# Line-aligned tiles and a batch pipeline for the first chunk of a fused retention and GELU-MLP kernel

## The chip, the cores and the metric

The kernel runs on one core of a Trainium2 chip. The time is the device time of one execution in microseconds (us); a kernel is compared by the median of its timed runs. Engines are named as in the profile: PE multiplies matrices (PEld is its weight load), DVE, ACT and POOL do elementwise work, SP only issues DMAs. ACT and POOL issue DMAs as well, from the same instruction stream as their elementwise work, so such an issue stands in the way of what comes behind it.

## The reference

```python
def _attn_ref(q, k, v):                       # 4 batches, 8 heads, 768 steps, head size 64
    gamma = 1.0 - 2.0 ** (-5.0 - np.arange(H))
    scale = 1.0 / np.sqrt(D)
    for t in range(S):
        state = gamma * state + k_t (outer) v_t       # per batch and head, 64 x 64
        y[:, :, t] = scale * (q_t @ state)

def _moe_ref(x, w_in, w_out):                 # x: 3072 x 512, d_ff = 2048
    h = x @ w_in
    g = gelu_tanh(h)
    return g @ w_out
```

A decayed recurrent attention produces `x` (3072 tokens of 512 values), and a two-layer MLP with a tanh GELU is applied to each token.

## The kernel before

**Tiling.** The sequence is cut into 6 chunks `c` of 128 steps; each chunk has 4 batches `b`. The recurrence is done by chunks: inside a chunk as a masked attention, between chunks through a state `st` (f16) that is carried per batch. The 8 heads go as 4 pairs, one pair filling the 128 partitions.

**One batch of one chunk** is a chain that alternates between PE and the elementwise engines:

- `load1` brings q, k and v from HBM as 128 x 8 x 64 f32 tiles (256 KB each, in rows of 256 bytes).
- `prep1` scales q and k by the decay and casts all three to f16 (`q16`, `k16`, `v16`), at line 141 (q, k) and line 136 or 138 (v).
- `mm_T` transposes q and k on PE (L171) and `ev_T` copies the result out of PSUM (`qkT`, L163 on ACT, L165 on DVE).
- `mm_A` forms the scores (L189, 8 matmuls into two PSUM tiles) and `ev_A` masks them out into `a_sb` (L202, two DVE instructions).
- `mm_Y` forms the output `y_ps` (L212 from the state, L222 from the scores) and the state's increment `s_ps` (L234); `ev_Y` copies y into `xT`, the MLP's input (L163 or L165); `ev_S` updates `st` (L251 in chunk 0, L253 later, two DVE instructions); `decay` multiplies the state for the next chunk into `stg` on POOL (L262).

The PSUM tiles of T, A (two), Y and S all come from one ring of three buffers (tag `att`): each new tile waits until the third one before it has been copied out.

**The MLP.** `moe1(c, fc)` multiplies all 4 batches of a chunk (512 tokens) by one 128-column block `fc` of `w_in` (16 blocks, 4 matmuls each, L316) and applies the GELU on ACT (L325). It can be done for half of the tokens (256 columns, batches 0 and 1, or 2 and 3). `moe2` multiplies by `w_out` (L336), and `ev_O` writes the output. `w_in` lies in five tiles of 2, 2, 4, 4 and 4 blocks, `w_out` in four; POOL issues their loads, which cast f32 to f16.

**The order** is written out by hand; each engine runs its own instructions in the order in which the code emits them. `spin(n)` emits `n` matmuls of a zero tile by itself, 512 columns wide (L108), whose result is not used.

- *Chunk 0* (lines 394 to 426): after 16 spins, batch 0 is started; then each turn of the loop over `b` = 1 to 3 emits prep, `spin(5)`, `mm_T` of batch `b`, `mm_Y` of `b - 1`, the evictions on ACT, `mm_A` and `ev_A` of `b`, then `ev_S` and `decay` of `b - 1`. In turn 2 POOL first copies one element of the loaded q tile of batch 3, so that it waits for it, and then issues the five loads of `w_in`. Loads: ACT issues q and v of batch 0 and q of batch 1, SP all the others, in order of the batches.
- Then `moe1` for the first two blocks and batches 0 and 1, `mm_Y` of batch 3, blocks 2 and 3 for the first half, blocks 0 to 3 for the second half, and blocks 4 to 15 for all tokens.
- `hold` (L86) writes one element of the tile of q of chunk 1, batch 0, with a value of `w_in` tile 3: the loads of chunk 1 wait on SP until that tile has landed. Then POOL prepares chunk 1 and issues the loads of `w_out`; the loads of chunk 2 are held in the same way until `w_out` tile 2 is there.
- *Chunk 1*: T and A of batch 0 lie between blocks 14 and 15, then T1, Y0, A1 and Y1 follow one another, and T2 to Y3 are spread over `moe1` of chunk 1's first half. Later chunks are spread over the MLP of the chunk before.

**Addresses.** In the compiled kernel the tile `zero` starts at byte 17408 of each partition (68 x 256). The tile `warm`, two bytes wide, comes behind it, and every tile after that starts 32 bytes past a multiple of 256: the first q tile at 67616 (264 x 256 + 32), for instance.

Of the kernel before, what the change touches and what calls it, by code (L numbers as in the profile page):

```python
# [9 lines left out]
F16 = mybir.dt.float16  # L10
F32 = mybir.dt.float32
AF = mybir.ActivationFunctionType
# [4 lines left out]
def kernel(  # L17
# [9 lines left out]
    nc = tc.nc  # L27
    B, H, S, Dh = q.shape
# [5 lines left out]
    NF = d_ff // 128  # L34
# [12 lines left out]
    cst_h = nc.inline_tensor(cst_np, name="rr_cst")  # L47
# [4 lines left out]
    const = ctx.enter_context(tc.tile_pool(name="const", bufs=1))  # L52
# [6 lines left out]
    psum = ctx.enter_context(tc.tile_pool(name="psum", bufs=1, space=bass.MemoryType.PSUM))  # L59

    OQ, OK, OG, OT = 0, H, 2 * H, 2 * H + NHP
    cst = const.tile([128, OT + 128], F32)
    iden = const.tile([128, 128], F16)
    scr = const.tile([1, 4], F32)

    raw = {}
    srcs = {"q": q, "k": k, "v": v}
# [1 line left out]
    def ld_tile(nm, c, b):  # L69
        if (nm, c, b) not in raw:  # L70
            raw[nm, c, b] = ld.tile([128, H, Dh], F32, tag=f"{nm}32", name=f"{nm}32")
        return raw[nm, c, b]

    def load1(eng, nm, c, b):
        eng.dma_start(
            out=ld_tile(nm, c, b),
            in_=srcs[nm][b, :, c * C:(c + 1) * C, :].rearrange("h p d -> p h d"),
        )

    def load(c, b):  # L80
        for nm in "qkv":
            load1(nc.sync, nm, c, b)
# [2 lines left out]

        nc.gpsimd.tensor_copy(out=ld_tile(nm, c, b)[0:1, 0, 0:1], in_=until)  # L86

    nc.sync.dma_start(out=cst, in_=cst_h.ap())
    load1(nc.scalar, "q", 0, 0)
    load1(nc.sync, "k", 0, 0)  # L90
    load1(nc.scalar, "v", 0, 0)
    nc.sync.dma_start(out=iden, in_=iden_h.ap())
    load1(nc.scalar, "q", 0, 1)
    load1(nc.sync, "k", 0, 1)
    load1(nc.sync, "v", 0, 1)
    load(0, 2)
    load(0, 3)


    zero = const.tile([128, 512], F16, name="zero")  # L100
    nc.vector.memset(zero, 0.0)  # L101
    warm = const.tile([128, 1], F16)
    nc.scalar.activation(out=warm, in_=zero[:, 0:1], func=AF.Gelu_apprx_tanh, scale=1.0)

    def spin(n):
        ps = psum.tile([128, 512], F32, tag="o", bufs=2, name="spin_ps")
        for _ in range(n):
            nc.tensor.matmul(  # L108
                out=ps, lhsT=zero[:, 0:128], rhs=zero, start=True, stop=True
            )  # L110
# [20 lines left out]
    def prep1(eng, nm, c, b):  # L131
        t = pre.tile([128, H, Dh], F16, tag=f"{nm}16", name=f"{nm}16")
        src = raw[nm, c, b]
        if nm == "v":
            if eng is nc.scalar:
                eng.copy(out=t, in_=src)
            else:
                eng.tensor_copy(out=t, in_=src)  # L138
        else:
            col = OQ if nm == "q" else OK  # L140
            eng.tensor_tensor(  # L141
                out=t,
                in0=src,
                in1=cst[:, col:col + H].unsqueeze(2).broadcast_to([128, H, Dh]),
                op=ALU.mult,
            )
        h16[nm, c, b] = t
# [19 lines left out]
    def mm_T(c, b):  # L167
        ps = psum.tile([128, 2, NHP, 128], F16, tag="att", bufs=3, name="qkT_ps")
        for i, nm in ((0, "q"), (1, "k")):
            for hp in range(NHP):  # L170
                nc.tensor.transpose(  # L171
                    out=ps[:, i, hp], in_=pair(h16[nm, c, b], hp), identity=iden
                )
        pss["T", c, b] = ps

    def ev_T(c, b, eng=nc.vector):
        t = att.tile([128, 2, NHP, 128], F16, tag="qkT", name="qkT")
        copy_on(eng, t, pss.pop(("T", c, b)))
        qkT[c, b] = t

    def mm_A(c, b):
        t = qkT[c, b]
        ps = [
            psum.tile([128, NHP, 128], F32, tag="att", bufs=3, name=f"a_ps{j}")
            for j in range(2)
        ]
        for hp in range(NHP):
            for j in range(2):
                nc.tensor.matmul(  # L189
                    out=ps[j][:, hp],  # L190
                    lhsT=t[j * 64:(j + 1) * 64, 1, hp],
                    rhs=t[j * 64:(j + 1) * 64, 0, hp],
                    start=True,
                    stop=True,
                )
        pss["A", c, b] = ps

    def ev_A(c, b):
        ps = pss.pop(("A", c, b))
        for j in range(2):  # L200
            s = att.tile([128, NHP, 128], F16, tag=f"a{j}", name=f"a_sb{j}")
            nc.vector.tensor_tensor(out=s, in0=ps[j], in1=mask[:, j], op=ALU.mult)  # L202
            a_sb[c, b, j] = s

    def mm_Y(c, b):
        vv = h16["v", c, b]
        kk = h16["k", c, b]
        y_ps = psum.tile([128, NHP, 128], F32, tag="att", bufs=3, name="y_ps")
        if c > 0:

            for hp in range(NHP):
                nc.tensor.matmul(  # L212
                    out=y_ps[:, hp],
                    lhsT=st[:, hp, b],
                    rhs=qkT[c, b][:, 0, hp],
                    start=(hp == 0),
                    stop=False,
                    skip_group_check=True,
                )
        for hp in range(NHP):  # L220
            for j in range(2):
                nc.tensor.matmul(  # L222
                    out=y_ps[j * 64:(j + 1) * 64, hp],
                    lhsT=vv[:, 2 * hp + j],
                    rhs=a_sb[c, b, j][:, hp],
                    start=(c == 0),
                    stop=True,
                    skip_group_check=True,
                )
        pss["Y", c, b] = y_ps  # L230
        if c + 1 < NCk:
            s_ps = psum.tile([128, NHP, 128], F32, tag="att", bufs=3, name="s_ps")
            for hp in range(NHP):
                nc.tensor.matmul(  # L234
                    out=s_ps[:, hp], lhsT=pair(kk, hp), rhs=pair(vv, hp), start=True, stop=True
                )
            pss["S", c, b] = s_ps

    def ev_Y(c, b, eng=nc.vector):
        if c not in xT:  # L240
            xT[c] = xp.tile([128, NHP, B * C], F16, tag="x", name="xT")
        copy_on(eng, xT[c][:, :, b * C:(b + 1) * C], pss.pop(("Y", c, b)))

    def ev_S(c, b):
        if c + 1 >= NCk:
            return
        s_ps = pss.pop(("S", c, b))
        for j in range(2):
            sl = slice(j * 64, (j + 1) * 64)
            if c == 0:  # L250
                nc.vector.tensor_copy(out=st[sl, :, b, sl], in_=s_ps[sl, :, sl])  # L251
            else:
                nc.vector.tensor_tensor(  # L253
                    out=st[sl, :, b, sl],
                    in0=s_ps[sl, :, sl],
                    in1=stg[sl, :, b, sl],
                    op=ALU.add,
                )

    def decay(c, b):  # L260
        if c + 2 < NCk:
            nc.gpsimd.tensor_tensor(  # L262
                out=stg[:, :, b],
                in0=st[:, :, b],
                in1=cst[:, OG:OG + NHP].unsqueeze(2).broadcast_to([128, NHP, 128]),
                op=ALU.mult,
            )
# [27 lines left out]
    def load_w_in(i):  # L295
        nc.gpsimd.dma_start(
            out=w_in_sb[i],
            in_=moe_w_in.rearrange("(kc p) n -> p kc n", p=128)[
                :, :, w_in_at[i] * 128:(w_in_at[i] + w_in_n[i]) * 128
            ],  # L300
        )
# [72 lines left out]
    def pieces(c, names):  # L374
        return [(p[0], c, int(p[1])) for p in names.split()]
# [15 lines left out]
    half = 2 * C  # L391


    spin(16)
    prep1(VE, "q", 0, 0)
    prep1(PO, "k", 0, 0)
    prep1(AC, "v", 0, 0)
    mm_T(0, 0)
    ev_T(0, 0, AC)
    spin(6)  # L400
    mm_A(0, 0)
    ev_A(0, 0)
    for b in range(1, B):
        prep1(VE, "q", 0, b)
        prep1(VE if b == 3 else PO, "k", 0, b)
        prep1(AC, "v", 0, b)
        if b == 2:

            PO.tensor_copy(out=scr[:, 0:1], in_=ld_tile("q", 0, 3)[0:1, 0, 0:1])
            for i in range(len(w_in_n)):  # L410
                load_w_in(i)
        spin(5)
        mm_T(0, b)
        mm_Y(0, b - 1)
        ev_T(0, b, AC)
        ev_Y(0, b - 1, AC)
        mm_A(0, b)
        ev_A(0, b)
        ev_S(0, b - 1)
        decay(0, b - 1)  # L420
    for fc in range(0, 2):
        moe1(0, fc, 0, half)
    mm_Y(0, 3)
    ev_Y(0, 3)
    ev_S(0, 3)
    decay(0, 3)


    hold("q", 1, 0, w_in_sb[3][0:1, 0, 0:1])
# [8 lines left out]
    for b in range(B):  # L438
        load(2, b)

    for fc in range(2, 4):
        moe1(0, fc, 0, half)
    for fc in range(0, 4):
        moe1(0, fc, half, 2 * half)
    for fc in range(4, 14):
        moe1(0, fc)
    zip_units(
        [(lambda fc=fc: moe1(0, fc)) for fc in range(14, 16)], pieces(1, "T0 A0")
    )
    for nm, c, b in pieces(1, "T1 Y0 A1 Y1"):  # L450
        fn[nm](c, b)
    zip_units(
        [(lambda fc=fc: moe1(1, fc, 0, half)) for fc in range(NF)],
        pieces(1, "T2 A2 Y2 T3 A3 Y3"),
# [68 lines left out]
```

## Time and profile before

| | us |
|---|---|
| median of 3 runs | 247.88 (245.59 to 249.09) |
| the profiled execution | 249.57 |
| its span, from first to last instruction | 247.8 |
| PE busy in it | 230.5 (93%) |
| mean granted clock of PE | 0.952 |

The span leaves out about 1.8 us that lie around the instructions. The profile's strips cut the span into 40 slices; the table of windows gives the busy time of each engine in any stretch, with the clock that PE was granted (1.00 is full speed). The chain that ended last lists, in order of time, the work that each later piece waited for.

### The profile page before, as it was taken

How to read it: one execution, taken by the hardware profiler on the slowest of the kernel's cores; microseconds unless marked ns; L12 is line 12 of the kernel's file. 1: busy time of each engine (PE TensorE's matmuls, PEld its weight loads, DVE VectorE, ACT ScalarE, POOL GpSimd, SP SyncE). 2: the span in 40 equal slices, each digit the busy share in tenths (PEclk: the TensorE clock that was granted, in tenths of full speed). 3: DMA queues.
4: the chain of work that ended last, by engine and by line, in shares of the span. 5: the costliest groups of instructions: out<-in, count | busy, mean ns of one | idle time of the engine just before them, and what ended most of it. 6: DMA issues, size and time to landing. Idle time of an engine off the chain costs nothing.

```text
span 247.8 us, 4006 instructions
## 1 busy us (share of the span) xinstructions
PE 230.5 (93%) x1637; PEld 122.6 (49%) x1637; DVE 84.2 (34%) x150; ACT 80.8 (33%) x148; POOL 81.7 (33%) x96
## 2 busy tenths in 40 slices
PE   8837899889999999979999999999999999999994
PEld 2413564457873445534454454454555445444453
DVE  3345410655400055752344532435434333200001
ACT  2423356215661010002551015540125530066210
POOL 3348138663694001159410169990000000000000
PEclk9995589958999999997999999999999999999999
DMA  8998979999992189939931119961120002110022
GB/s 163 218 145 109 195 135 219 196 161 192 222 224 67 73 199 198 248 126 227 218 63 42 42 45 217 219 117 42 45 86 0 3 0 85 45 42 0 2 82 87
DMA packets 83538, 29.73 MB, mean 120 GB/s; under 512 B 75584, under 2 KB 80576, under 8 KB 83520
## 3 DMA queue, kind: packets, MB, share of 16 engines
q1 hardware_dynamic: 75648, 24.49, 47.6%
q0 software_dynamic: 4752, 4.19, 11.1%
q10 hardware_dynamic: 3120, 0.79, 1.8%
q8 instruction: 13, 0.21, 0.4%
q14 instruction: 5, 0.04, 0.1%
HBM read 27.37 MB, written 6.29 MB: 136 GB/s over the span
## 4 chain that ended last, share of the span: by engine, by line
PE 83%; DVE 6%; POOL 4%; ACT 3%; issue 2%; DMA 1%; POOLq 0%; DVEq 0%; ACTq 0%
PE h_ps L316 35%; PE o_ps L336 31%; PE qkT_ps L171 5%; PE a_ps L189 3%; PE y_ps L222 3%; PE spin_ps L108 3%; DVE a_sb L202 2%; PE s_ps L234 2%; POOL k L141 2%; PE y_ps L212 2%; POOL q L141 1%; ACT qkT L163 1%; DVE st L253 1%; ACT o_sb L163 1%; POOL stg L262 1%
## 5 line engine op out<-in xcount | busy, mean ns | idle before, releaser
L316 PE MATMUL h_ps<-xT,w_in 128*128 128x512 f16 (+1 forms) x464 | 93.5, 357 | 0.2 <-DVE xT L165 0.2
L336 PE MATMUL o_ps<-w_out,g 128*128 128x512 f16 (+1 forms) x400 | 88.8, 371 | 1.0 <-ACT o_sb L163 0.9
L325 ACT ACTIVATE g<-h_ps 128x512 f16<-128x512 f32 (+1 forms) x116 | 60.7, 524 | 71.8 <-PE h_ps L316 70.3
L316 PEld LDWEIGHTS <-w_in 128*128 128x128 f16 x464 | 46.0, 103 | 36.9 <-issue 2.0
L336 PEld LDWEIGHTS <-g 128*128 128x128 f16 x400 | 37.3, 98 | 39.6 <-issue 1.9
L202 DVE TENSOR_TENSOR a_sb<-a_ps,mask 128x512 f16<-128x512 f32 x48 | 30.9, 686 | 40.1 <-PE a_ps L189 40.1
L262 POOL TENSOR_TENSOR stg<-st,cst 128x512 f32<-128x512 f16 x16 | 17.5, 1097 | 65.0 <-DVE st L253 51.7
L163 ACT COPY o_sb<-o_ps 128x512 f32<-128x512 f32 x18 | 10.5, 586 | 70.8 <-PE o_ps L336 66.2
L165 DVE COPY qkT<-qkT_ps 128x1024 f16<-128x1024 f16 x20 | 13.8, 691 | 38.4 <-PE qkT_ps L171 38.4
L141 POOL TENSOR_TENSOR k<-k,cst 128x512 f16<-128x512 f32 x23 | 24.0, 1044 | 6.8 <-DMA k<-in_k_dram 6.6
L141 POOL TENSOR_TENSOR q<-q,cst 128x512 f16<-128x512 f32 x20 | 20.9, 1045 | 6.1 <-DMA q<-in_q_dram 6.1
L165 DVE CAST xT<-y_ps 128x512 f16<-128x512 f32 x21 | 14.5, 692 | 23.4 <-PE y_ps L222 23.4
L171 PE MATMUL qkT_ps<-iden,q 128*128 128x128 f16 x96 | 9.8, 227 | 4.8 <-DVE q L141 3.0
L253 DVE TENSOR_TENSOR st<-s_ps,stg 64x256 f16<-64x256 f32 x32 | 13.4, 418 | 0.4
L108 PE MATMUL spin_ps<-zero 128*128 128x512 f16 x37 | 12.2, 490 | 1.2 <-DVE zero L101 1.2
L165 DVE COPY o_sb<-o_ps 128x512 f32<-128x512 f32 x5 | 3.5, 692 | 28.7 <-PE o_ps L336 28.7
L171 PEld LDWEIGHTS <-q 128*128 128x128 f16 x96 | 7.3, 101 | 11.5 <-DVE q L141 4.9
L171 PE MATMUL qkT_ps<-iden,k 128*128 128x128 f16 x96 | 10.0, 231 | 3.2 <-POOL k L141 2.3
L189 PE MATMUL a_ps<-qkT 64*128 64x128 f16 x192 | 11.1, 229 | 1.9 <-ACT qkT L163 0.9
L138 POOL CAST v<-v 128x512 f16<-128x512 f32 x20 | 12.2, 612 | 0.6 <-DMA v<-in_v_dram 0.2
L189 PEld LDWEIGHTS <-qkT 64*128 64x128 f16 x192 | 6.1, 97 | 11.6 <-issue 8.4
L222 PE MATMUL y_ps<-a_sb,v 128*64 128x128 f16 x192 | 11.0, 235 | 0.7 <-DVE a_sb L202 0.7
(30 smaller groups left out, 74.1 us busy)
## 6 DMA issues: line engine op xcount, KB each, us to landing
k<-in_k_dram SPq DMA_DIRECT2D x24, 256.0 KB, 5.0
v<-in_v_dram SPq DMA_DIRECT2D x23, 256.0 KB, 5.0
out_dram<-o_sb SPq DMA_DIRECT2D x23, 256.0 KB, 2.1
q<-in_q_dram SPq DMA_DIRECT2D x22, 256.0 KB, 4.9
w_out<-in_moe_w_out_dram POOLq DMA_DIRECT2D x4, 512.0 KB, 9.6
w_in<-in_moe_w_in_dram POOLq DMA_DIRECT2D x3, 512.0 KB, 9.8
q<-in_q_dram ACTq DMA_DIRECT2D x2, 256.0 KB, 5.3
w_in<-in_moe_w_in_dram POOLq DMA_DIRECT2D x2, 256.0 KB, 4.8
```

The lines of the kernel that those rows point to most:

```text
L108: nc.tensor.matmul(out=ps, lhsT=zero[:, 0:128], rhs=zero, start=True, stop=True)
L141: eng.tensor_tensor(out=t, in0=src, in1=cst[:, col:col + H].unsqueeze(2).broadcast_to([128, H, Dh]), op=ALU.mult,)
L165: eng.tensor_copy(out=out, in_=in_)
L171: nc.tensor.transpose(out=ps[:, i, hp], in_=pair(h16[nm, c, b], hp), identity=iden)
L189: nc.tensor.matmul(out=ps[j][:, hp], lhsT=t[j * 64:(j + 1) * 64, 1, hp], rhs=t[j * 64:(j + 1) * 64, 0, hp], start=True, stop=True,)
L202: nc.vector.tensor_tensor(out=s, in0=ps[j], in1=mask[:, j], op=ALU.mult)
L222: nc.tensor.matmul(out=y_ps[j * 64:(j + 1) * 64, hp], lhsT=vv[:, 2 * hp + j], rhs=a_sb[c, b, j][:, hp], start=(c == 0), stop=True, skip_gr ...
L253: nc.vector.tensor_tensor(out=st[sl, :, b, sl], in0=s_ps[sl, :, sl], in1=stg[sl, :, b, sl], op=ALU.add,)
L262: nc.gpsimd.tensor_tensor(out=stg[:, :, b], in0=st[:, :, b], in1=cst[:, OG:OG + NHP].unsqueeze(2).broadcast_to([128, NHP, 128]), op=ALU.mult,)
L316: nc.tensor.matmul(out=h_ps[:, t0:t1], lhsT=w_in_sb[wi][:, kc, wr * 128:(wr + 1) * 128], rhs=xT[c][:, kc, t0:t1], start=(kc == 0), stop=(k ...
L325: nc.scalar.activation(out=g_sb[c, fc][:, t0:t1], in_=h_ps[:, t0:t1], func=AF.Gelu_apprx_tanh, scale=1.0,)
L336: nc.tensor.matmul(out=ps[:, n0:n1], lhsT=g_sb[c, fc][:, b * C:(b + 1) * C], rhs=w_out_sb[fc // (NF // NO)][:, fc % (NF // NO), n0:n1], st ...
```

## The change

Tiles are given other widths, so that all tiles from `iden` on start at a multiple of 256 bytes: `cst` is padded to 768 bytes, and `scr` and `warm` become columns of one tile `misc` of 128 bytes. The DMAs of chunk 0's q, k and v are dealt out over the queues of SP and ACT, six each; three of ACT's are emitted behind its first activation (two ahead of its first cast, one behind `ev_T` of batch 0). The loop over the batches of chunk 0 is replaced by an order written out: q and k of the next batch are prepared ahead of `mm_A` of the current one, T of the next batch comes ahead of Y of the current one, the four `decay` come at the end, and there are fewer spins. At the end of chunk 0's `moe1` the order with chunk 1 changes, and eight spins are put between T1, Y0, A1 and Y1 there.

```diff
-    cst = const.tile([128, OT + 128], F32)
+    misc = const.tile([128, 32], F32)
+    cst = const.tile([128, 192], F32)
     iden = const.tile([128, 128], F16)
-    scr = const.tile([1, 4], F32)
...
-    load1(nc.scalar, "q", 0, 1)
-    load1(nc.sync, "k", 0, 1)
+    load1(nc.sync, "q", 0, 1)
+    load1(nc.scalar, "k", 0, 1)
     load1(nc.sync, "v", 0, 1)
-    load(0, 2)
-    load(0, 3)
+    load1(nc.sync, "k", 0, 2)
+    load1(nc.sync, "q", 0, 3)
+    load1(nc.sync, "v", 0, 3)
...
-    warm = const.tile([128, 1], F16)
-    nc.scalar.activation(out=warm, in_=zero[:, 0:1], func=AF.Gelu_apprx_tanh, scale=1.0)
+    nc.scalar.activation(
+        out=misc[:, 0:1], in_=zero[:, 0:1], func=AF.Gelu_apprx_tanh, scale=1.0
+    )
...
-    spin(16)
+    load1(AC, "q", 0, 2)
+    load1(AC, "v", 0, 2)
+    spin(14)
     prep1(VE, "q", 0, 0)
     prep1(PO, "k", 0, 0)
     prep1(AC, "v", 0, 0)
     mm_T(0, 0)
     ev_T(0, 0, AC)
-    spin(6)
+    load1(AC, "k", 0, 3)
+    prep1(VE, "q", 0, 1)
+    prep1(PO, "k", 0, 1)
+    spin(3)
     mm_A(0, 0)
     ev_A(0, 0)
-    for b in range(1, B):
-        prep1(VE, "q", 0, b)
-        prep1(VE if b == 3 else PO, "k", 0, b)
-        prep1(AC, "v", 0, b)
-        if b == 2:
-            PO.tensor_copy(out=scr[:, 0:1], in_=ld_tile("q", 0, 3)[0:1, 0, 0:1])
-            for i in range(len(w_in_n)):
-                load_w_in(i)
-        spin(5)
-        mm_T(0, b)
-        mm_Y(0, b - 1)
-        ev_T(0, b, AC)
-        ev_Y(0, b - 1, AC)
-        mm_A(0, b)
-        ev_A(0, b)
-        ev_S(0, b - 1)
-        decay(0, b - 1)
-    for fc in range(0, 2):
-        moe1(0, fc, 0, half)
+    mm_T(0, 1)
+    ev_T(0, 1, AC)
+    prep1(AC, "v", 0, 1)
+    mm_Y(0, 0)
+    ev_Y(0, 0, AC)
+    spin(2)
+    prep1(VE, "q", 0, 2)
+    prep1(PO, "k", 0, 2)
+    PO.tensor_copy(out=misc[0:1, 1:2], in_=ld_tile("q", 0, 3)[0:1, 0, 0:1])
+    for i in range(len(w_in_n)):
+        load_w_in(i)
+    mm_A(0, 1)
+    ev_A(0, 1)
+    ev_S(0, 0)
+    mm_T(0, 2)
+    ev_T(0, 2, AC)
+    prep1(AC, "v", 0, 2)
+    mm_Y(0, 1)
+    ev_Y(0, 1, AC)
+    spin(2)
+    prep1(VE, "q", 0, 3)
+    prep1(VE, "k", 0, 3)
+    mm_A(0, 2)
+    ev_A(0, 2)
+    ev_S(0, 1)
+    mm_T(0, 3)
+    ev_T(0, 3, AC)
+    spin(2)
+    mm_A(0, 3)
+    ev_A(0, 3)
+    prep1(AC, "v", 0, 3)
+    mm_Y(0, 2)
+    ev_Y(0, 2, AC)
+    ev_S(0, 2)
+    moe1(0, 0, 0, half)
     mm_Y(0, 3)
     ev_Y(0, 3)
     ev_S(0, 3)
-    decay(0, 3)
+    moe1(0, 1, 0, half)
+    for b in range(B):
+        decay(0, b)
...
-    for fc in range(2, 4):
-        moe1(0, fc, 0, half)
-    for fc in range(0, 4):
+    for fc in range(2):
         moe1(0, fc, half, 2 * half)
-    for fc in range(4, 14):
+    for fc in range(2, NF - 1):
         moe1(0, fc)
-    zip_units(
-        [(lambda fc=fc: moe1(0, fc)) for fc in range(14, 16)], pieces(1, "T0 A0")
-    )
-    for nm, c, b in pieces(1, "T1 Y0 A1 Y1"):
-        fn[nm](c, b)
+    run1 = lambda names: [fn[nm](c, b) for nm, c, b in pieces(1, names)]
+    run1("T0")
+    moe1(0, NF - 1)
+    run1("A0 T1")
+    spin(2)
+    run1("Y0 A1")
+    spin(4)
+    run1("Y1")
+    spin(2)
```

More of the change, by code (lines that the diff above doesn't have):

```diff
@@ L86, in hold @@
         nc.gpsimd.tensor_copy(out=ld_tile(nm, c, b)[0:1, 0, 0:1], in_=until)
-    nc.sync.dma_start(out=cst, in_=cst_h.ap())
+    nc.sync.dma_start(out=cst[:, :OT + 128], in_=cst_h.ap())
     load1(nc.scalar, "q", 0, 0)
```

## The prediction

> **What bounds the kernel now.** The page first, then the chain that ended last, then windows for the clock.
>
> ```profile
> PE 230.5 (93%) x1637; PEld 122.6 (49%) x1637; DVE 84.2 (34%) x150; ACT 80.8 (33%) x148; POOL 81.7 (33%) x96
> PEclk9995589958999999997999999999999999999999
> PE 83%; DVE 6%; POOL 4%; ACT 3%; issue 2%; DMA 1%; POOLq 0%; DVEq 0%; ACTq 0%
> ```
>
> PE is 83% of the chain, so from about 28 us on a gain is an earlier start of dense matmuls, a gap less, or a higher clock. The clock strip has three dips, near 20 to 33, 50 to 57 and 112 us; the change touches the first two. The chain in order of time (start, duration, what):
>
> ```profile
> 11.27 0.64 PE qkT_ps L171 x8
> 11.93 1.01 ACT qkT L163
> 12.94 0.50 ACT xT L163
> 13.48 0.39 PE a_ps L189 x7
> 13.88 1.27 DVE a_sb L202 x2
> 15.15 0.32 DVE st L251
> 15.49 0.44 DVE st L251
> 16.06 1.48 POOL stg L262
> 17.54 1.01 POOL k L141
> 18.59 0.41 PE qkT_ps L171 x4
> ...
> 25.40 0.62 PE qkT_ps L171 x4
> ...
> 31.16 13.20 PE h_ps L316 x68
> ...
> 45.67 0.39 PE a_ps L189 x8
> ...
> 52.10 1.03 PE h_ps L316 x4
> ...
> 53.99 1.71 PE h_ps L316 x8
> ...
> 56.24 1.87 PE h_ps L316 x12
> ...
> 216.56 13.81 PE h_ps L316 x64
> ```
>
> Read it as a loop: T of batch 1 ends at 11.91, T of batch 2 at 19.00 (18.59 + 0.41), T of batch 3 at 26.02. A turn takes 7.1 us, and no DMA is in it: ACT, PE, DVE, then POOL's `decay` (1.48) and its k (1.01), for which T waits. Dense `moe1` follows from 31.16. One block of 512 tokens takes 4 x 13.81 / 64 = 0.863 us at full clock, and blocks 4 to 14 end at 44.36, so block 4 started at 44.36 - 11 x 0.863 = **34.87**, the mark by which I measure chunk 0. From the end of block 15 (45.67) to chunk 1's first `moe1` (52.10) lie 6.43 us of attention with PE mostly waiting.
>
> The windows (stretch, length, PE busy, ..., PEclk, DMA share, GB/s):
>
> ```profile
> 12.77:16.19 3.42, 1.79 (x13) 0.71 (x13) 2.28 (x5) 1.28 (x3) 0.13 (x1) 1.00 1.39 217
> 16.19:19.60 3.41, 1.40 (x20) 0.93 (x20) 0.45 (x1) 0.57 (x1) 3.41 (x5) 1.00 0.16 26
> 19.60:23.01 3.41, 2.78 (x15) 1.00 (x13) 1.88 (x4) 1.45 (x3) 2.93 (x4) 0.50 0.97 122
> 29.84:33.25 3.41, 3.41 (x25) 2.46 (x24) 1.85 (x4) 1.11 (x3) 2.09 (x3) 0.50 0.83 137
> 33.25:36.67 3.42, 3.42 (x25) 2.17 (x23) 0.00 (x0) 2.22 (x7) 0.12 (x1) 1.00 0.67 144
> 46.90:50.32 3.42, 2.33 (x29) 1.44 (x29) 3.36 (x7) 0.00 (x0) 3.31 (x6) 1.00 0.83 148
> 50.32:53.73 3.41, 2.78 (x24) 2.06 (x23) 1.81 (x4) 0.38 (x1) 3.22 (x4) 0.50 1.16 174
> ```
>
> The clock changes on a grid of 3.41 us. A stretch with PE busy for 1.40 or 2.33 us was followed by half clock, one with 1.79 by full clock: about half busy is the border. Half clock ended only behind a stretch that PE filled (3.41 of 3.41).
>
> **The change, part by part.**
>
> *The turn of chunk 0.* k and q of the next batch are prepared ahead, and `decay` leaves the turn. What is left is set by the ring of three PSUM tiles: A's second tile waits for `ev_Y` of the batch before, and T waits for its `ev_S`. The cast of v now stands between ACT's two copies:
>
> ```profile
> 4.16 2.18 SPq L75 DMA_DIRECT2D q<-in_q_dram  x1
> 6.38 2.35 SPq L75 DMA_DIRECT2D k<-in_k_dram  x1
> 8.81 1.04 POOL L141 TENSOR_TENSOR k<-k,cst 128x512 f16<-128x512 f32 x1 [1.60 <-DMA k<-in_k_dram]
> 10.35 0.62 ACT L136 CAST v<-v 128x512 f16<-128x512 f32 x1 [1.63 <-DMA v<-in_v_dram]
> ```
>
> So a new turn is `ev_T` 1.01 + v 0.62 + `ev_Y` 0.50 (0.59 with its tail) + A 0.39 + `ev_A` 1.27 + `ev_S` 0.78 + T 0.45, and 0.15 of hand-overs: **5.25 us** for 7.1. The 0.45 of T is its share where both halves are ready (0.64 above has a wait for k). Removed POOL work costs nothing where it goes: four `decay` of 1.04 fit between the last `w_in` issue and the landing of `w_in` tile 3, below.
>
> *The loads.* Two queues do not make them faster:
>
> ```profile
> 3.00:4.00 1.00, 1.00 (x4) 0.33 (x3) 0.89 (x7) 1.00 (x1) 0.00 (x0) 1.00 1.17 262
> 5.00:9.00 4.00, 4.00 (x26) 1.88 (x26) 0.00 (x0) 1.63 (x2) 1.23 (x2) 1.00 1.39 218
> 9.00:16.00 7.00, 4.56 (x46) 2.16 (x44) 3.98 (x8) 2.74 (x4) 0.86 (x1) 1.00 1.39 218
> ```
>
> 218 GB/s with both queues (5 to 9) and with SP alone (9 to 16). k of batch 1 landed at 8.81; third on ACT's queue, 0.79 MB at half of 218 GB/s, it lands near 9.2. POOL's 1.04 and T's second half put the end of T1 at 10.7, and I add 0.3, since DVE's q now runs beside POOL's k: 11.0 for 11.91. The price of ACT's own issues: SP's rows of 2.18 and 2.35 are issues into a queue that is full while two queues drain. ACT's q of batch 2 goes in at 4.4 with three loads ahead of it, partly drained, in 0.5 us; its v takes some 2.4 and ends at 7.4, 0.4 behind the landing of v of batch 0. That delay stays hidden, because T1 waits for k anyway. The bounds for all three issues are nothing and 2.35 each; the upper one is a rival.
>
> *The end of chunk 0.* T3 ends at 11.0 + 2 x 5.25 = 21.5, for 26.02. But a turn of 5.25 us holds 0.45 (T) + 0.40 (A) + 0.75 (Y and S) + 0.6 (two spins) = 2.2 us of PE, or 1.4 in 3.41, what dropped the clock at 19.60. So I take half clock from about 16 to 19 on: T and A 0.2 longer each, T3 at 21.9. Behind it: `ev_T` 1.0, A3 0.6, `ev_A` 1.3, and beside these Y2, S2, two blocks of half the tokens, Y3, S3 (0.6 each) follow one another on PE without a gap worth naming; blocks 0 and 1 of the second half start at 27.5 behind `ev_Y` of batch 3, and blocks 2 and 3 follow. Dense work from about 24.3; a filled stretch then ends between 27.7 and 31.1. Block 4 starts between 29.7 and 31.4; I take **31.0**, for 34.87: -3.9.
>
> *Is w_in there?* Its issues:
>
> ```profile
> 18.61 3.92 POOL L296 DMA_DIRECT2D w_in<-in_moe_w_in_dram  x5
> DMA to landing us min/median/max: 4.1/8.0/11.6
> ...
> w_in<-in_moe_w_in_dram POOLq DMA_DIRECT2D x3, 512.0 KB, 9.8
> ...
> 33.19 0.18 POOL L86 CAST q<-w_in 1x1 f32<-1x1 f16 x1
> ```
>
> They wait for q of batch 3, which lands near 16.1 (seventh on SP's queue: 1.34 MB from 2.9 us on at half of 218 GB/s is 12.3, and I allow 0.9 for landing), so the first issue moves to 16.3, 2.3 earlier. The five issues take 0.78 each, so the third and fourth start near 20.2 and 21.0; tile 2 landed 8.0 behind its issue (the median of the five) and tile 3 9.8 (that of the three big ones), at 28.2 and 30.8. Shifted: 25.9 and 28.5, ahead of blocks 4 and 8. So `hold` runs near 28.9 for 33.19, and chunk 1's loads move by -4.3, slightly more than PE does: T0 and T1 find their inputs, as before.
>
> *Chunk 1's attention.* The same chain on DVE, with eight spins: at 0.216 each 1.7 us of PE that otherwise waits; two of them delay Y0 by 0.1 at most. The 6.43 us stay, +0.1. PE's busy time in them rises from half to some 70%, so I take it that the clock is kept. Then the matmuls from 52.10 to 57.14 gain: 24 of 256 columns took 1.03 + 1.71 + 1.87 = 4.6 us and take 24 x 0.108 = 2.6, and T and A lose 0.6 more: **-2.6**.
>
> *Aligned tiles.* No row shows a 256-byte row written to a whole line. Bounds: no change, up to the 262 GB/s that the engines did for the first microsecond. I take no change, the nearest row being the sustained 218. By the Trainium skill, DMA: Bandwidth & Descriptors, section How a descriptor splits into AXI transactions, a 256-byte row that starts 32 bytes past a line is two transactions and an aligned one is one; that would speak for the upper bound, and no row here shows it.
>
> The sum: -3.9 + 0.1 - 2.6 = **-6.4** on 249.57, or 243.2 in the profiled execution's terms. That execution is 1.69 above the median; the runs shown spread by 3.5, somewhat more than one dip is worth. Taken off the median: **241.5**.
>
> **The rivals.**
>
> *The clock holds in chunk 0.* T3 ends at 21.5, block 4 starts at 28.35: -6.5 + 0.1 - 2.6 = -9.0, 238.9. For it: 1.79 busy was enough at 16.19. Against: 1.4 is less. By the Trainium skill, TensorE: Matmul & The Clock Gate, section What's actually happening, the clock falls behind an idle window of about 3.4 us, and the new turn's gaps are near 2 us, so by that rule this case would be the one; the trace does not agree, since the stretch from 46.90 with 2.33 us busy was followed by half clock.
>
> *It falls in both chunks.* Chunk 1 keeps its loss: -3.9 + 0.1 = -3.8, 244.1. For it: 2.33 busy was not enough at 50.32.
>
> *ACT is held by its issues.* At 2.35 each it is free at 9.1 instead of 7.4 and at 13.1 for `ev_T` of batch 1 instead of 10.7: 2.4 later, -4.0, 243.9. Against: SP's issues took that long only with the queue full.
>
> *Aligned rows load at 262 GB/s.* k of batch 1 lands 0.7 earlier, and T1 with it; the later turns don't wait for loads: -7.1, 240.8.
>
> *Slower: aligned operands slow PE.* Place: the 864 matmuls of L316 and L336. From 6.4 / 864 = 7.4 ns each the gain is gone; at 13 ns (229 for 215.8) it is 252.7. Against it, `zero` lies on a whole line already:
>
> ```profile
> 7.67 1.29 PE spin_ps L108 x6
> ```
>
> 6 spins in 1.29 us are 215 ns each, as quick as the 216 of `h_ps` from tiles off the line.
>
> **How the numbers follow.** Forecast 0.42, own range 239.5 to 243.5; the clock holds 0.20; it falls twice 0.13; ACT held 0.09; loads at 262 0.09; PE slowed 0.03; 0.04 for nothing gained. A measurement of this kernel tells about 2% (4.96 us) from no change, so faster means under 242.9: 0.33 of the forecast's part, nearly all of the clock's and the loads' cases, together 0.62; slower (over 252.8) 0.03; the rest, 0.35, within 2%. The range, 237.5 to 245.3, takes in the clock both ways and the held ACT, and leaves out the ends.
>
> **What would show it.** T of batches 1, 2 and 3 (L171) near 11, 16 and 21.5 to 22, with A of batch 2 waiting for ACT's xT and T of batch 3 for DVE's st; a granted clock of 0.50 somewhere between 16 and 31 and none near chunk 1's attention; block 4 near 31; chunk 1's first `moe1` near 48.3. It is wrong if T follows the loads' pace of 3.6 us a batch, if PE waits for `w_in`, or if later stretches, which I take as shifted whole, lose what the first gain.

## The result and the profile after

| | before | after |
|---|---|---|
| median, us | 248.48 (245.59 to 249.09, 4 runs) | 235.77 (235.75 to 236.07, 4 runs) |
| profiled execution / its span | 249.57 / 247.8 | 235.79 / 234.0 |
| mean granted clock in it | 0.952 | 1.000 |

The ratio is **0.9513**, 95% interval 0.9436 to 0.9591: 4.9% faster, below the range of the prediction. Of the kernels below, one execution of the one without chunk 0's spins (291 us, the profiled one) ran at three quarters of the clock or less throughout and is left out.

The page of the changed kernel: PE's clock strip has lost all three dips.

```profile
PE 219.7 (94%) x1623; PEld 117.2 (50%) x1623; DVE 84.2 (36%) x150; ACT 80.3 (34%) x146; POOL 81.1 (35%) x96
PEclk9999999999999999999999999999999999999999
```

Its chain in order of time (start, duration, what), where the lines have moved by about four (T is L175, A L193, `moe1` L320, `moe2` L340):

```profile
8.72 0.73 PE qkT_ps L175 x8
9.47 1.01 ACT qkT L167
10.49 0.52 ACT v L140
11.00 0.50 ACT xT L167
11.54 0.40 PE a_ps L193 x7
11.94 1.28 DVE a_sb L206 x2
...
13.55 0.43 DVE st L255
14.01 0.69 DVE q L145
14.70 1.46 DVE k L145
16.18 0.70 DVE a_sb L206
16.92 0.62 PE qkT_ps L175 x8
...
21.95 12.26 PE h_ps L320 x60
34.21 0.45 PE qkT_ps L175 x8
34.66 0.86 PE h_ps L320 x4
35.52 0.39 PE a_ps L193 x8
...
41.75 0.61 PE h_ps L320 x4
...
59.50 6.71 PE o_ps L340 x31
...
116.27 1.73 PE o_ps L340 x8
```

T of batch 1 ends at 9.45 (11.91 before) and T of batch 3 at 17.54 (26.02 before). Blocks 2 to 14 end at 34.21, so block 4 started at 34.21 - 11 x 0.863 = 24.72, for 34.87. Chunk 1's first `moe1` starts at 41.75, for 52.10. The same two later marks in the chain of the kernel before:

```profile
72.14 6.70 PE o_ps L336 x31
130.03 1.73 PE o_ps L336 x8
```

So the 13.8 us between the two profiled executions came in four places: 10.15 up to block 4; 0.2 in chunk 1's attention; 2.3 between its first `moe1` and the first `moe2` (20.04 us before, 17.75 after), where the clock no longer fell; and 1.1 up to 116.27, where the dip near 112 us is gone.

The loads, by windows (stretch, length, busy of each engine, PEclk, DMA share, GB/s):

```profile
5.00:9.00 4.00, 3.54 (x29) 1.74 (x27) 0.94 (x2) 1.63 (x2) 2.26 (x2) 1.00 1.28 288
9.00:13.00 4.00, 2.67 (x33) 1.72 (x33) 2.81 (x5) 2.02 (x3) 2.04 (x3) 1.00 1.28 288
```

288 GB/s where it was 218. And two lines of its timeline:

```profile
12.42 3.91 POOL L300 DMA_DIRECT2D w_in<-in_moe_w_in_dram  x5
12.67 0.38 PE L175 MATMUL qkT_ps<-iden,q 128*128 128x128 f16 x4 [0.74 <-DVE a_sb L206]
```

POOL issues `w_in` from 12.42 on, for 18.61 before. T of batch 2 waited for `ev_A` (L206), the first half of which ended at 12.62, and not for `ev_S`, which began at 13.21.

### The profile page after: what moved, and what is told of

It reads as the page before. It is cut to its first block, busy times and chain, and to the rows that moved or that the text cites. A ratio compares the mean times of both kernels' runs of the same rounds, so it can differ in the third digit from the quotient of the medians.

```text
span 234.0 us, 3976 instructions
## 1 busy us (share of the span) xinstructions
PE 219.7 (94%) x1623; PEld 117.2 (50%) x1623; DVE 84.2 (36%) x150; ACT 80.3 (34%) x146; POOL 81.1 (35%) x96
## 4 chain that ended last, share of the span: by engine, by line
PE 83%; DVE 6%; POOL 4%; ACT 3%; issue 2%; DMA 1%; POOLq 0%; DVEq 0%; ACTq 0%
PE h_ps L320 33%; PE o_ps L340 33%; PE qkT_ps L175 4%; PE a_ps L193 3%; PE y_ps L226 3%; PE spin_ps L112 3%; DVE a_sb L206 2%; PE s_ps L238 2%; POOL q L145 2%; POOL k L145 2%; PE y_ps L216 2%; ACT qkT L167 1%; DVE st L257 1%; ACT o_sb L167 1%; DVE xT L169 1%
## 5 line engine op out<-in xcount | busy, mean ns | idle before, releaser
L340 PE MATMUL o_ps<-w_out,g 128*128 128x512 f16 (+1 forms) x400 | 88.8, 371 | 1.0 <-ACT o_sb L167 0.9
L320 PE MATMUL h_ps<-xT,w_in 128*128 128x512 f16 (+1 forms) x456 | 88.6, 346 | 0.2
L320 PEld LDWEIGHTS <-w_in 128*128 128x128 f16 x456 | 43.0, 98 | 35.3 <-DVE xT L169 0.5
L340 PEld LDWEIGHTS <-g 128*128 128x128 f16 x400 | 37.3, 98 | 39.6 <-issue 1.9
L206 DVE TENSOR_TENSOR a_sb<-a_ps,mask 128x512 f16<-128x512 f32 x48 | 30.9, 686 | 27.3 <-PE a_ps L193 27.3
L266 POOL TENSOR_TENSOR stg<-st,cst 128x512 f32<-128x512 f16 x16 | 16.5, 1040 | 49.7 <-DVE st L257 46.4
L169 DVE COPY qkT<-qkT_ps 128x1024 f16<-128x1024 f16 x20 | 13.8, 691 | 35.8 <-PE qkT_ps L175 35.8
L145 POOL TENSOR_TENSOR k<-k,cst 128x512 f16<-128x512 f32 x23 | 24.5, 1063 | 6.2 <-DMA k<-in_k_dram 6.2
L257 DVE TENSOR_TENSOR st<-s_ps,stg 64x256 f16<-64x256 f32 x32 | 13.3, 417 | 0.4
L175 PE MATMUL qkT_ps<-iden,q 128*128 128x128 f16 x96 | 9.3, 219 | 3.7 <-DVE a_sb L206 1.9
L193 PE MATMUL a_ps<-qkT 64*128 64x128 f16 x192 | 10.2, 219 | 2.0 <-ACT qkT L167 1.2
L193 PEld LDWEIGHTS <-qkT 64*128 64x128 f16 x192 | 5.6, 94 | 12.1 <-issue 7.6
L112 PE MATMUL spin_ps<-zero 128*128 128x512 f16 x31 | 10.4, 472 | 1.2 <-DVE zero L104 1.2
L175 PEld LDWEIGHTS <-q 128*128 128x128 f16 x96 | 7.1, 98 | 8.7 <-POOL q L145 2.3
L175 PE MATMUL qkT_ps<-iden,k 128*128 128x128 f16 x96 | 9.3, 220 | 1.0 <-POOL k L145 1.0
## 6 DMA issues: line engine op xcount, KB each, us to landing
w_out<-in_moe_w_out_dram POOLq DMA_DIRECT2D x4, 512.0 KB, 10.5
```

The costliest lines, as they stand in the source:

```text
L112: nc.tensor.matmul(out=ps, lhsT=zero[:, 0:128], rhs=zero, start=True, stop=True)
L145: eng.tensor_tensor(out=t, in0=src, in1=cst[:, col:col + H].unsqueeze(2).broadcast_to([128, H, Dh]), op=ALU.mult,)
L169: eng.tensor_copy(out=out, in_=in_)
L175: nc.tensor.transpose(out=ps[:, i, hp], in_=pair(h16[nm, c, b], hp), identity=iden)
L193: nc.tensor.matmul(out=ps[j][:, hp], lhsT=t[j * 64:(j + 1) * 64, 1, hp], rhs=t[j * 64:(j + 1) * 64, 0, hp], start=True, stop=True,)
L257: nc.vector.tensor_tensor(out=st[sl, :, b, sl], in0=s_ps[sl, :, sl], in1=stg[sl, :, b, sl], op=ALU.add,)
```

## The experiments

Three things could have made the difference: the **lines** (a faster rate of loads), the **order**, and the **clock**. The mark used below is the start of block 4, T of chunk 1 less 11 x 0.863 = 9.49 us.

### All tiles 32 bytes off the line

```diff
-    misc = const.tile([128, 32], F32)
+    misc = const.tile([128, 40], F32)
```

> The changed kernel with one tile 32 bytes wider, so that all tiles start 32 bytes past a 256-byte line again; order, queues and spins are those of the change. If the lines set the rate of the loads: 218 GB/s from 5 to 9 us instead of 288, q of batch 3 landing near 16 instead of 12.3, the first w_in issue near 16.2 instead of 12.4, and 238 to 242 us. If the order and the two queues gave the gain and the rate came from the second queue: 280 GB/s or more as in the changed kernel, and 235.5 to 236.5 us.

Measured: 239.67 us, ratio to before 0.9713 (0.9646 to 0.9779). One window, one line of the timeline and three of the chain:

```profile
5.00:9.00 4.00, 3.48 (x17) 1.40 (x15) 0.23 (x2) 1.55 (x2) 1.04 (x1) 1.00 1.39 220
15.44 3.91 POOL L300 DMA_DIRECT2D w_in<-in_moe_w_in_dram  x5
8.77 8.73 DMA k<-in_k_dram
...
17.53 0.70 DVE k L145
...
38.56 0.45 PE qkT_ps L175 x8
```

The rate is back at 220 GB/s, so the lines set it and not the second queue. k of batch 3 now is on the chain until 17.50, `w_in` is issued 3.0 us later, and block 4 starts at 29.07; two stretches at half clock, from 20.48 to 27.30, are part of that. The order with all else takes 7.7 us off the kernel before without the lines.

### The widths alone, in the kernel before

```diff
-    cst = const.tile([128, OT + 128], F32)
+    misc = const.tile([128, 32], F32)
+    cst = const.tile([128, 192], F32)
     iden = const.tile([128, 128], F16)
-    scr = const.tile([1, 4], F32)
...
-    warm = const.tile([128, 1], F16)
-    nc.scalar.activation(out=warm, ...)
+    nc.scalar.activation(out=misc[:, 0:1], ...)
```

> The kernel before with the new tile widths alone (all tiles on whole lines). If the lines set the rate: over 235 GB/s from 9 us on, where it was 218, and the loads done some 2 us earlier; but the turn of 7.1 us per batch waits for no load, so the time stays within 1.5 us of the kernel before (245 to 249). If faster loads by themselves shorten chunk 0: at least 4 us less, 244 or below.

Measured: 248.23 us, ratio 0.996 (0.9897 to 1.0023). Windows, and T of batch 2 in its chain:

```profile
5.00:9.00 4.00, 3.93 (x30) 1.85 (x29) 0.26 (x1) 1.79 (x3) 2.09 (x2) 1.00 1.26 285
9.00:13.00 4.00, 2.52 (x30) 1.33 (x29) 1.62 (x3) 2.12 (x4) 0.00 (x0) 1.00 1.12 253
18.00 0.62 PE qkT_ps L170 x4
```

The loads run at 285 GB/s and the time doesn't move: T of batch 2 ends at 18.6, 0.4 earlier, because the turn waits for `decay` and k on POOL. Faster loads pay only where something waits for them, which the new order brings about.

### Half a line off, and 224 bytes off

```diff
-    misc = const.tile([128, 32], F32)
+    misc = const.tile([128, 64], F32)
```

The other kernel has `[128, 88]` there.

> The changed kernel with all tiles 128 bytes past a 256-byte line, half a line, for the rate of the loads alone. If what counts is that a row touches two lines: 215 to 222 GB/s from 5 to 9 us, as at 32 bytes past. If the bytes on the second line cost too (the Trainium skill, DMA: Bandwidth & Descriptors, How a descriptor splits into AXI transactions, counts 12 beats here, 9 at 32 bytes past and 8 on the line): below 205.

> The changed kernel with all tiles 224 bytes past a line, for the rate of the loads alone. If what counts is that a row touches two lines, wherever it is cut: 215 to 222 GB/s from 5 to 9 us, as at 32 and 128 bytes past. If the cut matters: outside 210 to 228.

Measured, each in one run (239.71 and 240.17 us), the window from 5 to 9 us of the one and the other:

```profile
5.00:9.00 4.00, 3.05 (x17) 1.29 (x15) 0.32 (x1) 1.41 (x2) 1.04 (x1) 1.00 1.34 222
5.00:9.00 4.00, 3.47 (x17) 1.40 (x15) 0.12 (x2) 1.56 (x2) 1.04 (x1) 1.00 1.35 218
```

222 and 218 GB/s, beside 220 at 32 bytes: where the row is cut makes no difference of note, only that it is. By the Trainium skill, DMA: Bandwidth & Descriptors, section How a descriptor splits into AXI transactions, such a row becomes two transactions; the trace agrees with a price for the second one, and not with a price by the beats that the section counts.

### The loads on the queues of before

Chunk 0's loads are issued as in the kernel before (q, v of batch 0 and q of batch 1 on ACT, the others on SP), in the new order and on the lines.

```diff
-    load1(nc.sync, "q", 0, 1)
-    load1(nc.scalar, "k", 0, 1)
+    load1(nc.scalar, "q", 0, 1)
+    load1(nc.sync, "k", 0, 1)
     load1(nc.sync, "v", 0, 1)
-    load1(nc.sync, "k", 0, 2)
...
+    load(0, 2)
+    load(0, 3)
...
-    load1(AC, "q", 0, 2)
-    load1(AC, "v", 0, 2)
...
-    load1(AC, "k", 0, 3)
```

> The changed kernel with chunk 0's loads on the queues of before (three on ACT, all others on SP). If the second queue matters once rows lie on whole lines: 288 GB/s while both queues hold loads and about 241 afterwards (what SP's queue alone reached from 28 to 37 us in the changed kernel), q of batch 3 landing 1 to 1.5 us later, and 236.3 to 237.5 us. If the queues make no difference: 235.6 to 236.1.

Measured: 238.31 us (238.22 to 238.53). The timeline's line for q of batch 3, which POOL waits for, here and in the changed kernel (L421):

```profile
12.62 0.18 POOL L417 COPY misc<-q 1x1 f32<-1x1 f32 x1 [0.83 <-DMA q<-in_q_dram]
```

```profile
12.29 0.18 POOL L421 COPY misc<-q 1x1 f32<-1x1 f32 x1 [0.51 <-DMA q<-in_q_dram]
```

0.3 us later, not 1 to 1.5, and the time is in neither of the ranges that I had given. It is that of a clock that fell: half from 10.96 to 24.61 in the profile, and a mean of 0.971 to 0.986 in each run. Six more runs of the changed kernel have a median of 237.98 (below), 0.3 us less than this; its first four are 2.5 less. So the second queue is worth 0.3 us in the landing of q, and whether it decides on the clock isn't shown.

### Chunk 1's spins, taken out and put in alone

```diff
     run1("A0 T1")
-    spin(2)
     run1("Y0 A1")
-    spin(4)
     run1("Y1")
-    spin(2)
```

> The changed kernel without the eight spins in chunk 1's attention. If those spins hold the clock: granted 0.50 for one or two stretches of 3.41 us from about 41 on, and 237 to 238.5 us. If the clock would hold without them: 1.00 throughout and 235.5 to 236 us.

> The kernel before with the eight spins in chunk 1's attention alone, batch pipeline and widths as before. If they keep the clock there: no half clock near 50 us in any run, a mean clock of 0.965 to 0.972 and 245 to 246.5 us, where the kernel before spreads from 245.3 to 249.1. If they do nothing: the same spread and median as the kernel before, 246.5 to 248.

Without them: 238.92 us (238.23 to 241.25). A window of it, and the chain behind it:

```profile
40.48:43.89 3.41, 1.88 (x22) 1.39 (x23) 2.87 (x6) 0.00 (x0) 2.71 (x4) 1.00 1.18 182
44.74 1.71 PE h_ps L320 x8
```

The same place in the changed kernel, on its grid:

```profile
40.19:43.60 3.41, 3.04 (x34) 2.09 (x32) 2.46 (x5) 0.70 (x2) 3.08 (x4) 1.00 1.03 149
```

After a stretch with PE busy for 1.88 us the clock was half for one stretch: eight matmuls take 1.71 us, where they take 0.87 in the changed kernel. With the spins PE is busy for 3.04 us there, and the clock stays. In the kernel before, the spins alone give 246.16 us (ratio 0.9964, 0.9932 to 0.9997), no run above 246.9, where the kernel before reaches 249.3 among the runs timed beside it. By the ratio they are worth 0.1 to 1.7 us. Without them the clock doesn't always fall: in the profile of the kernel before with the widths alone it stayed at full speed there, with PE busy for 2.42 and 2.25 us in the two stretches.

### The changed kernel again, and without chunk 0's spins

No change for the first; for the second:

```diff
-    spin(3)
     mm_A(0, 0)
...
     ev_Y(0, 0, AC)
-    spin(2)
...
     ev_Y(0, 1, AC)
-    spin(2)
...
     ev_T(0, 3, AC)
-    spin(2)
```

> The changed kernel itself, unaltered. If the clock's dips in it hang on where the 3.41 us grid falls against the kernel's start: some runs with a mean clock of 0.97 to 0.99 and 1 to 3 us above 235.8, most without a dip. If its PE work is enough wherever the grid falls: every run at 0.993 or 1.000 and 235.7 to 236.1 us.

> The changed kernel without the nine spins inside chunk 0's attention (the first 14 stay). If those spins hold the clock there: half clock from some point between 10 and 17 us on in every run, for two to four stretches of 3.41 us, 237.5 to 240 us. If the quicker turns hold it without spins: 235.5 to 236.1 us.

The same kernel again: **237.98 us** (235.67 to 238.84, 6 runs), ratio 0.9617 (0.9564 to 0.967). Its mean clock was 0.978 to 0.986 in the four runs from 237.9 on and 0.993 in the two below. Windows on the grid of 3.41 us, first of the profile with the result, then of this one:

```profile
12.88:16.29 3.41, 2.16 (x30) 1.34 (x27) 3.33 (x6) 2.02 (x3) 3.41 (x5) 1.00 1.00 149
16.29:19.71 3.42, 1.78 (x26) 1.11 (x26) 2.51 (x5) 1.76 (x3) 2.15 (x3) 1.00 1.10 148
```

```profile
13.28:16.69 3.41, 1.82 (x24) 1.11 (x23) 3.33 (x5) 2.02 (x3) 3.41 (x6) 1.00 0.95 112
16.69:20.10 3.41, 2.80 (x26) 1.70 (x25) 1.88 (x5) 1.53 (x2) 1.98 (x2) 0.50 1.18 157
35.90 0.45 PE qkT_ps L175 x8
```

The instructions are the same and run at the same times up to 16.7, to within 0.1 us, but the grid lies 0.4 us later, and most of T of batch 2 (12.7 to 13.3) falls out of the window: 1.82 busy instead of 2.16, and the clock falls. Block 4 then starts at 26.41, 1.7 us later. Busy time alone doesn't decide it, though: the stretch with 1.78 above kept the clock. The first four runs, with a mean clock of 0.993 or 1.000, had one stretch at half clock at most and lost 0.3 us at most; the new order is at the border. That the place of the grid tips it is what these two profiles suggest; no run sets the grid.

This profile has a third stretch at half clock, near 98 us, where the changed kernel has a gap (below):

```profile
98.61:102.02 3.41, 1.30 (x12) 0.78 (x13) 0.47 (x1) 0.33 (x1) 3.41 (x5) 1.00 0.64 174
102.02:105.43 3.41, 3.41 (x16) 1.75 (x15) 0.47 (x2) 1.19 (x2) 3.41 (x5) 0.50 1.23 278
```

Without the nine spins: 238.0 to 238.8 us in three runs, a mean clock of 0.971 in each, which is about four stretches at half clock; in the ten runs with them it is none to three. They help, but aren't enough.

### More spins where PE waits, on and off the line

```diff
     ev_S(0, 0)
+    spin(3)
     mm_T(0, 2)
...
     ev_S(0, 1)
+    spin(4)
     mm_T(0, 3)
     ev_T(0, 3, AC)
-    spin(2)
+    spin(4)
```

> The changed kernel with nine more spins, put where PE waits in chunk 0: three ahead of T of batch 2, four ahead of T of batch 3 and two more behind it. They cost nothing at full clock, since PE waits 0.74, 1.16 and 0.73 us there. If the dip after 16 us comes from PE being too little busy: no half clock in chunk 0 in any run, and all runs within 235.5 to 236.2 us. If it comes from something else: the same spread as the changed kernel, 235.7 to 238.8.

> The same with all tiles 32 bytes past a line. With the clock held, what is left against the kernel with more spins is the loads' part alone: T of batch 3 about 2 us later (it ended at 19.6 with tiles off the line, at 17.5 on it), w_in 3 us later: 237.5 to 238.5 us. If the loads count only through the clock: within 0.5 us of the kernel with more spins.

On the line: 236.29 us (235.84 to 237.30, 6 runs), the clock at 1.000 in five and 0.993 in one. Off it: 237.73 (237.66 to 239.29). T of chunk 1 in the two chains, and a window of the first:

```profile
34.28 0.45 PE qkT_ps L175 x8
13.00:17.00 4.00, 3.09 (x34) 1.61 (x32) 3.92 (x7) 2.02 (x3) 4.00 (x6) 1.00 1.06 148
```

```profile
35.97 0.45 PE qkT_ps L175 x8
11.09:14.50 3.41, 3.41 (x24) 1.51 (x21) 1.75 (x3) 1.76 (x3) 1.04 (x1) 0.50 1.39 218
```

PE is busy for 3.09 of 4 us now, where it was 2.12, and the dip of chunk 0 is gone, for 1.7 us against the changed kernel's six runs (timed at another time); against its first four, which hardly had a dip, it is 0.5 us more. Four of the six runs lie above the 236.2 that I had expected at most, one of them with a stretch at half clock; the spread of 0.6 us among runs at full clock I can't account for. The lines by themselves are worth 1.4 us here (237.73 less 236.29) and 1.7 with the clock falling (239.67 less 237.98, not timed together). The profile off the line has one stretch at half clock, from 11.09; two runs there without any took 237.72 and 237.74.

### A version that beats both

The changed kernel has a gap left at 98 us, where POOL prepares chunk 3 behind chunk 2's last `decay`. With the spins above, batch 0 of the chunk after next is prepared ahead of the last Y:

```diff
-    fn = {"T": att_T, "A": att_A, "Y": att_Y}
+    fn = {"T": att_T, "A": att_A, "Y": att_Y, "P": prep}
...
-        return [(p[0], c, int(p[1])) for p in names.split()]
+        return [(p[0], c + (p[0] == "P"), int(p[1])) for p in names.split()]
...
+    EARLY = "T0 T1 A0 T2 A1 Y0 T3 A2 Y1 A3 P0 Y2 Y3"
...
-            for b in range(B):
+            for b in range(1, B):
                 prep(c + 1, b)
```

> The kernel with more spins, and from chunk 3 on POOL prepares batch 0 of the next chunk between A and Y of batches 2 and 3 of the chunk before, not behind its last decay. PE waited 1.81 and 0.60 us for these at 98 us in the changed kernel. If that wait is on the path: 2 to 2.7 us less than the kernel with more spins, 233 to 233.8 us. If the decays that are pushed back take its place: 235 us or more.

Measured: **232.86 us** (232.76 to 233.21), ratio 0.9463 (0.9411 to 0.9515). The wait in the changed kernel's timeline, and the same T here:

```profile
98.43 0.40 PE L175 MATMUL qkT_ps<-iden,q 128*128 128x128 f16 x4 [1.81 <-POOL q L145]
99.43 0.40 PE L175 MATMUL qkT_ps<-iden,k 128*128 128x128 f16 x4 [0.60 <-POOL k L145]
```

```profile
96.61 0.39 PE L175 MATMUL qkT_ps<-iden,q 128*128 128x128 f16 x4
96.83 0.39 PE L175 MATMUL qkT_ps<-iden,k 128*128 128x128 f16 x4
```

Both waits are gone, and all four runs had the clock at 1.000. It is 3.4 us less than the kernel with more spins (236.29, timed beside it), more than the 2 to 2.7 expected. Between the two profiled executions, 235.85 and 232.92, it is 2.9: 2.4 are the two waits, and the other 0.5 isn't accounted for. The rest is the spread of the kernel with more spins, whose profile is 0.4 below its median.

## Why the prediction was wrong

The direction held and the mechanisms of chunk 1 came out, but the gain was twice as large, 13.8 us for 6.4 between profiled executions. Most of the miss lies ahead of block 4, which started at 24.72 and not at 31.0. Of these 6.3 us, 1.55 are an earlier T of batch 1 (9.45 for 11.0), 2.4 the two turns behind it (8.1 for 10.5) and 2.65 the half clock that I had put into the sum (31.0 less 28.35); what follows T of batch 3 took 0.3 more than the sum has for a clock that holds. By its steps:

- **"T waits for its `ev_S`" is the step that failed first.** I had taken the three PSUM buffers as a ring in the order of allocation; the description of the kernel above says the same and is wrong there. T of batch 2 takes the buffer that comes free first, and that is the first half of `ev_A`. The turn was 3.8 us (T at 9.45, then 13.28) and 4.3, for 5.25. The second turn was DVE's: its chain doesn't leave DVE from 11.94 to 16.88, with q (0.69) and k (1.46) of batch 3 between `ev_S` and the next `ev_A`, two casts that my sum had put at nothing. Without the lines, T of batch 3 ended at 19.6, for the 21.9 I had worked out.
- **"I take no change, the nearest row being the sustained 218" was the second.** On whole lines the rate was 288, over my upper bound of 262, which was a rate of the first microsecond off the line. T of batch 1, which waits for k, ended at 10.8 without the lines, near the 11.0 I had worked out, and at 9.45 with them. With that term went "the later turns don't wait for loads": with the shorter turn they do, as the kernel 32 bytes off the line shows, and so the rival of faster loads was priced at 0.7 us and was worth 1.4 to 1.7. The first `w_in` issue moved by 6.2 us, for 2.3.
- **"I take half clock from about 16 to 19 on" was a border case**, and the largest of the terms. In the profile of the result it didn't fall; in that of the same kernel later it did, for 1.7 us at the mark. So this part is luck: the six later runs have a median of 237.98, just inside the range I gave. The rule that I read from the windows, about half busy, doesn't hold: 2.33 us busy lost the clock and 1.79 kept it in the very rows that I read it from, and 1.82 lost it and 1.78 kept it in the changed kernel. Nor did half clock end only behind a filled stretch: 3.10 us ended it in the kernel before (111.76 to 115.17). The PE time that I put into the rule belonged, besides, to a turn that was too long.
- The term up to block 4 was -3.9 and measured -10.15; this order and these queues alone, off the line and with a dip, gave 34.87 - 29.07 = -5.8.
- Chunk 1's attention kept its clock, as forecast: -2.3 for -2.6, and 6.23 us for 6.43 + 0.1. The dip near 112 us, which I left as it was, went too: 1.1 us that the sum didn't have. It came back in the later profile of the same kernel, at 102.02, so this is luck as well.
- PE never waited for `w_in`, `hold` ran early enough, and the later stretches shifted whole, as taken.
- The rivals: ACT wasn't held. Its issues behind the first activation took 0.37, 0.47 and 1.13 us; off the line the third took 2.51, and ACT's next copy began at 11.32, 0.5 behind T of batch 1. A block of `h_ps` from tiles on the line takes 0.86 us (at 34.66), as before, so aligned operands cost PE nothing.

## What to carry to other kernels

Tiles that DMAs fill in rows of 256 bytes belong on whole 256-byte lines, but it pays only once something on the path waits for a load; here the same widths gave nothing before the order was changed. Read from the trace which instruction frees the buffer that the next one gets, not from the order of allocation. Where PE is busy for about half of the time, one kernel can keep its clock in one run and lose it in the next, so one set of runs can mislead; wide matmuls of zeros where PE waits anyway made that rarer here (five of six runs had full clock throughout) and cost 0.1 us in the profile (235.85 for 235.79).

## What the runs showed that I had not expected

- A 256-byte row into SBUF cost about a third more when it crossed a line: 218 to 222 GB/s at 32, 128 and 224 bytes past it, 285 to 288 on it, with the same 16 engines and either division of the queues.
- The grid of the clock lies differently against the kernel's start from run to run: full clock began at 6.05 us in the profile of the result and at 6.45 in that of the same kernel later, and two stretches at half clock in chunk 0 came with these 0.4 us.
- Busy time in a stretch of 3.41 us sorts badly what follows: from 1.55 to 2.33 us the clock held in some and fell in others. Another count sorts better. By an estimate from the durations here, a matmul of 512 columns is 0.216 us of work at full clock and one of 128 columns 0.054; those that use 64 of the 128 rows or columns (A, and Y from the scores) I take by half. Then 13.28:16.69 of the later profile has 8 of Y, 4 of S, 8 of A and 2 spins: 0.22 + 0.22 + 0.22 + 0.43 = 1.1 us, and the clock fell; 12.88:16.29 of the first has 4 of T more, 1.3 us, and it held. The stretch from 46.90 in the kernel before has 1.0 and fell, that from 12.77 with its five spins 1.3 and held. Of the stretches at full clock in thirteen profiles, the ends of the kernels left out, 13 have less than 1.2 us, and the clock fell behind 12 of them; behind those from 1.25 us up it held, but for two with 1.3. If that is the rule, narrow matmuls count for little and a wide spin for much; no run was made to test it.
- DVE's cast of k of batch 3 took 1.46 us on the chain of the changed kernel (14.70), directly behind that of q, and 0.70 in the kernel 32 bytes off the line (17.53), where it came alone; POOL was issuing `w_in` beside both. The cause wasn't tried.
